# A gated mixer on one core: two x tiles and the first w_in blocks loaded in another order, and the left-over rows of the last four output tiles put in one 64-row stretch

## The chip, the core and the metric

The kernel runs on one core of a Trainium2 chip. The metric is the device time of one execution in microseconds (us); a kernel is run several times and the median counts. The profiles show one execution each. PE is TensorE's matmul stream and PEld its weight loads, DVE is VectorE, ACT is ScalarE, POOL is GpSimd, SP is SyncE. ACTq and SPq are the DMA issues of the ACT and SP queues.

## What is computed

S = 2048 rows, D = 512, F = 1376, half of it FH = 688, 32 heads of 16. All data are bf16. Cut to what matters:

```python
g = sigmoid((x * gate_w).sum(-1, keepdims=True))
# A: linear attention with softmax feature maps
q, k, v = split(x @ wqkv)
phi(t) = concat(softmax(t @ w_phi), softmax(-(t @ w_phi)))      # per head
a = (phi(q) @ (phi(k).T @ v)) / (phi(q) @ phi(k).sum(rows) + 1e-6) @ wo
# B: spatial gating
z = gelu(x @ w_in)
z1, z2 = z[:, :688], layernorm(z[:, 688:])
u = z1 * (w_sp @ z2 + b_sp[:, None])
b = u @ w_out
out = g * a + (1 - g) * b
```

## The kernel before

The 2048 rows are cut into 16 row tiles of 128. D is cut into four blocks of 128 (dt = 0..3), which TensorE contracts. `xT[:, dt, rows]` is x transposed, the stationary operand of nearly every matmul of the first half. The orders of PE and ACT are written out by hand (`tc.manual_schedule`), so both run in the order of the code; SP, POOL and DVE are ordered by the framework, in step with the code.

**Phase 1 (L321 to L338): z.** For each row tile, `z2_tile` multiplies x with the second half of w_in: eight matmuls (four dt, two column halves j of HF = 344 columns), accumulated in a two-bank PSUM tile `zp`. Column 344 of the second half is the gate logit, for which gate_w sits as a 689th column in `w_z2`. ACT then takes the gelu (L206). `z1_tile` does the same with the first half of w_in.

**The very beginning (`z2_first_two`, L215 to L257)** is written out apart, since nothing is in SBUF yet:

- L119 to L125 issue the first loads: SP takes x tile 0, then blocks dt = 0, 2, 3 of `w_z2`; ACT takes x tile 1 (so the two x tiles are loaded side by side), then block dt = 1, then gate_w into four rows of `gaterow`, which DVE has zeroed at L101.
- `warm_up` (L220) runs matmuls on constants into a bank that is overwritten later.
- `x_T` (L279) transposes blocks of an x tile on PE by a matmul with `ident`, and a copy on DVE (L287) or ACT (L284) takes them to `xT`.
- `one(tt, dt, j)` is one z matmul of row tile tt (L191). For j = 1 it is 345 columns wide, the gate's column among them.
- `gate_T` (L289) transposes gate_w on PE and DVE writes it into column 688 of all four blocks of `w_z2` (L292). A matmul that reads this column must wait for it.
- `z_part` (L229) does a part of the columns of half 1 for dt = 0: first 344 columns without the gate's, later that one column alone.

**Phase 2 (L573 to L595):** k, v, the key-value sums and the first halves of `w_sp @ z2` (`gg_half`, L452).

**Phase 3 (L597 to L608): output.** Step i of the loop does one `gg_half`, the attention of tile i + 1 (`attn_tile`, or `attn_tile_64` in 64-row matmuls), and `ba_step(i - 1)`, the output of a tile: `ba_attn` (four matmuls of 512 columns, from `oT`, L510) and `ba_spat` (five, from `uT`, L516), accumulated in one PSUM bank. u has 688 = 5*128 + 48 columns, so 48 left-over rows of its transpose remain. For them `uT` is padded, at one end for even tiles and at the other for odd ones, and `w_rem` holds the same 48 rows of w_out at its top and at its bottom, zeros between. `ba_rem` (L519) multiplies them: in the last step of a group of `BA_GROUPS` it runs once for each tile of the group, on rows 0 to 63 for even tiles and on rows 64 to 127 for odd ones (`halves`). Then `ba_store` scales each accumulator by 1 - g, on ACT (L531) or DVE (L527), and issues its DMA to `out`.

The groups are tiles 0-3, 4-7, 8-11 and 12-13. Tiles 14 and 15 come after the loop in `ba_tile` (L538): each does `ba_spat`, a `ba_rem` over all 128 rows, then `ba_attn`, then the store; tile 15 does so twice, for columns 0 to 383 and for columns 384 to 511. The PSUM banks of the outputs are four `acc_banks` in turn; `q_bank` and `g_bank` are two more, for `q_tile` and `gg_half`.

Of the kernel before, what the change touches and what calls it, by code (L numbers as in the profile page):

```python
# [14 lines left out]
P = 128  # L15
# [20 lines left out]
def kernel(  # L36
# [73 lines left out]
    for q in range(4):  # L110
        qs = slice(32 * q, 32 * q + 32)
        nc.vector.tensor_tensor(
            out=ident[qs, qs], in0=ramp[qs, 0, :], in1=ramp[qs, 1, :], op=ALU.is_equal)
    nc.gpsimd.memset(brow[:], 0.0)
    nc.gpsimd.memset(wphi[:], 0.0)
    def load_z2w(eng, dt):
        eng.dma_start(out=w_z2[:, dt, 0:FH], in_=w_in_v[:, dt, FH:F])

    nc.sync.dma_start(out=xs[:, 0, :], in_=x2[0:P, :])  # L119
    nc.scalar.dma_start(out=xs[:, 1, :], in_=x2[P:2 * P, :])  # L120
    load_z2w(nc.sync, 0)
    load_z2w(nc.scalar, 1)
    load_z2w(nc.sync, 2)
    nc.scalar.dma_start(out=gaterow[0:NDT, :], in_=gate_w.rearrange("(dt p) -> dt p", p=P))
    load_z2w(nc.sync, 3)  # L125
    scrap = early.tile([P, 1], BF16, name="scrap")
    nc.scalar.activation(
# [58 lines left out]
    def pq_tile(shape, dtype=FP32):  # L186
        return psF.tile(shape, dtype, name="pq", tag=next_turn("pq", 2))

    def z_one(zp, tt, wt, w, dt, j, skip=False):
        n = HF if j == 0 else w - HF  # L190
        nc.tensor.matmul(  # L191
            zp[:, j, 0:n], lhsT=xT[:, dt, tt * P:(tt + 1) * P],
            rhs=wt[:, dt, j * HF:j * HF + n],
            start=(dt == 0), stop=(dt == NDT - 1), skip_group_check=skip,
        )

    def z_mm(tt, wt, w):
# [17 lines left out]
    def z2_first_two():  # L215
        zps = [zp_tile() for _ in range(2)]
        tp1 = psA.tile([P, 2, P], BF16, name="tp1", tag=next_turn("zp", 3))
        turn["zp"] -= 1

        def warm_up(n, w=CH):  # L220
            for _ in range(n):
                nc.tensor.matmul(  # L222
                    zps[0][:, 1, 0:w], lhsT=nc.const_aps.tensor(1.0, [P, P], BF16),
                    rhs=nc.const_aps.tensor(1.0, [P, w], BF16), start=True, stop=True)

        def one(tt, dt, j):
            z_one(zps[tt], tt, w_z2, FH + 1, dt, j, skip=True)

        def z_part(tt, c0, c1, start):  # L229
            nc.tensor.matmul(  # L230
                zps[tt][:, 1, c0:c1], lhsT=xT[:, 0, tt * P:(tt + 1) * P],
                rhs=w_z2[:, 0, HF + c0:HF + c1], start=start, stop=False, skip_group_check=True)

        warm_up(6)
        warm_up(1, P)
        x_T(0, 0, 1, pq_tile([P, 1, P], BF16)[:, :, :])
        x_T(0, 1, NDT, pq_tile([P, 3, P], BF16)[:, :, :])
        x_T(1, 0, 2, tp1[:, :, :])
        x_T(1, 2, NDT, pq_tile([P, 2, P], BF16)[:, :, :], on_act=True)
        warm_up(2, P)  # L240
        one(0, 0, 0)
        z_part(0, 0, HF, True)
        one(0, 1, 0)
        one(1, 0, 0)
        gate_T()
        z_part(1, 0, HF, True)
        one(1, 1, 0)
        for tt in range(2):
            one(tt, 1, 1)
        for tt in range(2):  # L250
            one(tt, 2, 0)
            one(tt, 2, 1)
            z_part(tt, HF, HF + 1, False)
        for tt in range(2):
            one(tt, 3, 0)
            one(tt, 3, 1)
            z2_out(tt, zps[tt])  # L257
# [21 lines left out]
    def x_T(i, d0, d1, tp, on_act=False):  # L279
        for dt in range(d0, d1):  # L280
            nc.tensor.transpose(tp[:, dt - d0, :], xs[:, i, dt * P:(dt + 1) * P], ident[:, :])  # L281
        dst = xT[:, d0:d1, i * P:(i + 1) * P]
        if on_act:
            nc.scalar.copy(out=dst, in_=tp)  # L284
        else:
            with tc.high_priority():
                nc.vector.tensor_copy(out=dst, in_=tp)  # L287

    def gate_T():  # L289
        gt = pq_tile([P, NDT])  # L290
        nc.tensor.matmul(gt[:, :], lhsT=gaterow[:, :], rhs=ident[:, 0:NDT], start=True, stop=True)
        nc.vector.tensor_copy(out=w_z2[:, :, FH], in_=gt[:, :])  # L292
# [55 lines left out]
    def bank_tile(tag):  # L348
        return psM.tile([P, CH], FP32, name="mm", tag=tag)
# [158 lines left out]
    def ba_attn(acc, tt, start, stop, c0=0, c1=D):  # L508
        for g in range(NG):
            nc.tensor.matmul(acc, lhsT=oTs[tt][:, g, :], rhs=wo_t[:, g, c0:c1],  # L510
                             start=start and g == 0, stop=stop and g == NG - 1)

    def ba_spat(acc, tt, start, c0=0, c1=D):
        i = tt % 2
        for ft in range(5):
            nc.tensor.matmul(acc, lhsT=uTs[tt][:, i + ft, :], rhs=w_main[i][:, ft, c0:c1],  # L516
                             start=start and ft == 0, stop=False)

    def ba_rem(acc, tt, rows, stop, c0=0, c1=D):  # L519
        nc.tensor.matmul(  # L520
            acc, lhsT=uTs[tt][rows, 5 * (1 - tt % 2), :], rhs=w_rem[rows, c0:c1], start=False, stop=stop)

    def ba_store(acc, tt, c0, c1, on_dve):
        ob = work.tile([P, c1 - c0], BF16, name=f"ob{c1 - c0}", bufs=4 if c1 - c0 == D else 1)
        dst = out2[tt * P:(tt + 1) * P, c0:c1]
        if on_dve:
            nc.vector.tensor_scalar(  # L527
                out=ob[:, :], in0=acc, scalar1=g_inv[:, tt:tt + 1], scalar2=None, op0=ALU.mult)
            nc.sync.dma_start(out=dst, in_=ob[:, :])
        else:  # L530
            nc.scalar.activation(out=ob[:, :], in_=acc, func=AF.Copy, scale=g_inv[:, tt:tt + 1])  # L531
            nc.scalar.dma_start(out=dst, in_=ob[:, :])

    def acc_tile():
        acc_banks.append(acc_banks.pop(0))
        return bank_tile(acc_banks[-1])

    def ba_tile(tt, cuts=(0, D)):  # L538
        for h, (c0, c1) in enumerate(zip(cuts, cuts[1:])):
            acc = acc_tile()[:, 0:c1 - c0]  # L540
            ba_spat(acc, tt, True, c0, c1)
            ba_rem(acc, tt, slice(0, P), False, c0, c1)
            ba_attn(acc, tt, False, True, c0, c1)
            ba_store(acc, tt, c0, c1, h > 0)

    def ba_step(tt):
        group = next(g for g in BA_GROUPS if tt in g)
        accs[tt] = acc_tile()
        ba_attn(accs[tt][:, :], tt, True, False)
        ba_spat(accs[tt][:, :], tt, False)  # L550
        if tt == group[-1]:
            for t in group:
                ba_rem(accs[t][:, :], t, halves[t % 2], True)
            if tt + 2 < NT - 1:
                attn_tile_64(tt + 2)
            for t in group:
                ba_store(accs[t][:, :], t, 0, D, False)

    oTs = {}
    uTs = {}  # L560
    eqTs = {}
    accs = {}
    BA_GROUPS = [range(0, 4), range(4, 8), range(8, 12), range(12, 14)]
    Q_AT = (5, 7, 9, 11, 13, 15)
    ggs = [(tt, j) for tt in range(NT) for j in range(2)]

# [6 lines left out]
    with tc.manual_schedule(engines={mybir.EngineType.PE, mybir.EngineType.Activation}):  # L573
        ks = {0: k_tile(0)}
        kvacc = psM.tile([P, 8, P], FP32, name="kvacc", tag="kvat", bufs=1)
        pend = []
        for tt in range(NT):
            if tt + 1 < NT:
                ks[tt + 1] = k_tile(tt + 1)
            ek, rk = ks.pop(tt)  # L580
            pend.append((tt, ek, v_tile(tt, rk)))
            if len(pend) == 3:
                kv_acc(*pend.pop(0))
            gg_next(mm_tile())
            if tt == 7:
                w_main, w_rem, wo_t = load_out_weights()
            if tt in Q_AT:
                q_tile(Q_AT.index(tt), mm_tile())
        nc.scalar.activation(out=g_el[:, :], in_=glog[:, :], func=AF.Exp)
        nc.vector.tensor_scalar(out=g_1p[:, :], in0=g_el[:, :], scalar1=1.0, scalar2=None, op0=ALU.add)  # L590
        nc.vector.reciprocal(out=g_inv[:, :], in_=g_1p[:, :])
        for p_ in pend:
            kv_acc(*p_)
        kvz_evac()
        gg_next(mm_tile())  # L595
        nq = len(Q_AT)
        q_bank, g_bank, *acc_banks = [next_turn("mm", 6) for _ in range(6)]  # L597
        attn_tile(0)
        for i in range(NT - 1):
            if i + nq < NT:  # L600
                q_tile(i + nq, bank_tile(q_bank))
            gg_next(bank_tile(g_bank if i + nq < NT or i % 2 == 0 else q_bank))
            if i not in (4, 8, 12):
                attn_tile(i + 1)
            if i > 0:
                ba_step(i - 1)
        ba_tile(14)
        ba_tile(15, cuts=(0, 384, D))  # L608


# [28 lines left out]
```

The softmax here doesn't subtract the row's maximum and nothing guards it: scores larger than these inputs give would overflow.

## Time and profile before

| | us |
|---|---|
| median of 5 runs | 206.46 |
| lowest, highest | 206.21, 207.05 |
| the profiled execution | 206.21 |
| its span, first to last instruction | 204.5 |
| PE busy in it | 200.9 (98%) |
| PE weight loads | 120.2 (59%) |
| DVE, ACT, POOL busy | 129.6, 75.5, 45.6 |
| granted TensorE clock | 1.000 |

The page has the share of each engine, the span in 40 slices, the DMA queues, the chain of work that ended last, the groups of instructions by line, and the DMA issues with their median time to landing. Three further views are used: the timeline (instructions in order of time: start, duration of the piece, engine, line, operation, output and input, how many, and the idle time before it with what ended it), the chain of waits in order of time (start, length, what), and the answers for one tile, which give a DMA's time from issue to landing. [...]

### The profile page before, as it was taken

How to read it: one execution, taken by the hardware profiler on the slowest of the kernel's cores; microseconds unless marked ns; L12 is line 12 of the kernel's file. 1: busy time of each engine (PE TensorE's matmuls, PEld its weight loads, DVE VectorE, ACT ScalarE, POOL GpSimd, SP SyncE). 2: the span in 40 equal slices, each digit the busy share in tenths (PEclk: the TensorE clock that was granted, in tenths of full speed). 3: DMA queues.
4: the chain of work that ended last, by engine and by line, in shares of the span. 5: the costliest groups of instructions: out<-in, count | busy, mean ns of one | idle time of the engine just before them, and what ended most of it. 6: DMA issues, size and time to landing. Idle time of an engine off the chain costs nothing.

```text
span 204.5 us, 3998 instructions
## 1 busy us (share of the span) xinstructions
PE 200.9 (98%) x1559; PEld 120.2 (59%) x1559; DVE 129.6 (63%) x282; ACT 75.5 (37%) x123; POOL 45.6 (22%) x76
## 2 busy tenths in 40 slices
PE   8999999999999999999999999999999999999994
PEld 4666666655665555656565666555555555665642
DVE  4568484838977597979797689555566645633330
ACT  3566678795222333342424042222351126002222
POOL 3020202022523325424242442222204220200000
PEclk9999999999999999999999999999999999999999
DMA  6999799999999027941322229763557468542942
GB/s 201 254 212 147 87 145 282 182 290 221 250 258 204 3 38 195 275 93 23 69 53 40 51 38 119 150 120 70 98 157 80 91 114 181 68 96 53 148 89 79
DMA packets 89931, 27.22 MB, mean 133 GB/s; under 512 B 84184, under 2 KB 89912, under 8 KB 89912
## 3 DMA queue, kind: packets, MB, share of 16 engines
q1 hardware_dynamic: 87312, 24.59, 64.1%
q10 hardware_dynamic: 2600, 2.37, 4.3%
q8 instruction: 12, 0.20, 0.4%
q14 instruction: 7, 0.06, 0.1%
HBM read 4.15 MB, written 2.10 MB: 31 GB/s over the span
## 4 chain that ended last, share of the span: by engine, by line
PE 98%; DVE 0%; issue 0%
PE mm L455 37%; PE zp L191 18%; PE mm L356 14%; PE mm L516 9%; PE mm L510 7%; PE mm L396 7%; PE kvacc L412 2%; PE at L468 2%; PE zp L222 1%; PE mm L520 1%; PE zp L308 0%; PE at L479 0%; PE pq L281 0%; PE pq L308 0%; DVE ob L527 0%; PE zp L230 0%
## 5 line engine op out<-in xcount | busy, mean ns | idle before, releaser
L455 PE MATMUL mm<-z2all,wspT 128*128 128x344 bf16 x512 | 79.9, 309 | 0.0
L455 PEld LDWEIGHTS <-wspT 128*128 128x128 bf16 x512 | 49.0, 98 | 25.3
L191 PE MATMUL zp<-w_z,xT 128*128 128x344 bf16 (+1 forms) x254 | 38.1, 309 | 0.0
L360 ACT ACTIVATE eq<-mm 128x512 bf16<-128x512 f32 x32 | 17.4, 594 | 51.4 <-PE mm L356 25.7
L364 DVE TENSOR_REDUCE zs<-eq 128x64 f32<-128x1024 bf16 x16 | 19.5, 1220 | 20.1 <-ACT eq L360 20.1
L191 PEld LDWEIGHTS <-xT 128*128 128x128 bf16 x254 | 24.4, 98 | 12.0 <-issue 0.2
L360 ACT ACTIVATE ek<-mm 128x512 bf16<-128x512 f32 x32 | 17.3, 601 | 27.1 <-PE mm L356 27.1
L460 DVE SCALAR_TENSOR_TENSOR ucat<-mm,bT,z1all 128x344 bf16<-128x344 f32 x32 | 17.4, 544 | 15.1 <-PE mm L455 15.1
L373 POOL TENSOR_TENSOR eq<-eq,ratio 128x512 bf16<-128x512 bf16 x16 | 16.9, 1056 | 44.6 <-DVE ratio L372 36.6
L531 ACT ACTIVATE ob<-mm,g_inv 128x512 bf16<-128x512 f32 (+1 forms) x16 | 10.9, 680 | 32.4 <-PE mm L520 26.6
L364 DVE TENSOR_REDUCE zs<-ek 128x64 f32<-128x1024 bf16 x16 | 19.3, 1208 | 2.8 <-ACT ek L360 2.8
L516 PE MATMUL mm<-wspT,uT 128*128 128x512 bf16 (+2 forms) x85 | 20.1, 367 | 0.0
L356 PEld LDWEIGHTS <-xT 128*128 128x128 bf16 x128 | 12.2, 98 | 12.0
L373 POOL TENSOR_TENSOR ek<-ek,ratio 128x512 bf16<-128x512 bf16 x16 | 16.9, 1056 | 2.2 <-DVE ratio L372 1.7
L510 PE MATMUL mm<-wspT,oT 128*128 128x512 bf16 (+2 forms) x68 | 16.6, 366 | 0.0
L356 PE MATMUL mm<-wq_p,xT 128*128 128x512 bf16 x64 | 16.4, 379 | 0.0
L396 PE MATMUL mm<-wv_sb,xT 128*128 128x512 bf16 x64 | 16.4, 379 | 0.0
L356 PE MATMUL mm<-wk_p,xT 128*128 128x512 bf16 x64 | 16.3, 379 | 0.0
L209 DVE BATCH_NORM_STATS2 bn<-z2all 128x6 f32<-128x344 bf16 x32 | 14.9, 501 | 0.0
L206 ACT ACTIVATE z2all<-zp 128x688 bf16<-128x688 f32 x16 | 11.8, 743 | 7.3 <-PE zp L191 7.1
L261 ACT ACTIVATE z1all<-zp 128x688 bf16<-128x688 f32 x16 | 11.9, 743 | 5.1 <-PE zp L191 4.7
L516 PEld LDWEIGHTS <-uT 128*128 128x128 bf16 x85 | 8.1, 98 | 9.4 <-issue 0.2
(77 smaller groups left out, 143.0 us busy)
## 6 DMA issues: line engine op xcount, KB each, us to landing
out_dram<-ob ACTq DMA_DIRECT2D x15, 128.0 KB, 2.4
wspT<-in_B_w_out_dram SPq DMA_DIRECT2D x2, 640.0 KB, 4.9
w_z<-in_B_w_in_dram SPq DMA_DIRECT2D x2, 344.0 KB, 4.5
w_z<-in_B_w_in_dram SPq DMA_DIRECT2D x3, 172.0 KB, 3.3
wv_sb<-in_A_wqkv_dram SPq DMA_DIRECT2D x2, 256.0 KB, 2.8
wspT<-in_A_wo_dram SPq DMA_DIRECT2D x2, 256.0 KB, 4.0
uT<-ucat SPq DMA_TRANSPOSE x16, 2.8
eqT<-eq SPq DMA_TRANSPOSE x16, 3.9
```

Of the source, the lines that this page charges most:

```text
L191: nc.tensor.matmul(zp[:, j, 0:n], lhsT=xT[:, dt, tt * P:(tt + 1) * P], rhs=wt[:, dt, j * HF:j * HF + n], start=(dt == 0), stop=(dt == NDT ...
L209: nc.vector.bn_stats(out=bn6[:, tt, j, :], in_=z2v[:, j, :])
L261: nc.scalar.activation(out=z1all[:, tt, :].rearrange("p (j n) -> p j n", j=2), in_=zp[:, :, 0:HF], func=AF.Gelu_apprx_tanh,)
L356: nc.tensor.matmul(ps[:, :], lhsT=xT[:, dt, tt * P:(tt + 1) * P], rhs=w[:, dt, :], start=(dt == 0), stop=(dt == NDT - 1))
L360: nc.scalar.activation(out=e[:, :, a, :], in_=ps[:, :].rearrange("p (h f) -> p h f", f=DH), func=AF.Exp, scale=1.0 - 2.0 * a)
L364: nc.vector.tensor_reduce(out=z[:].rearrange("p h a -> p (h a)"), in_=e[:].rearrange("p h a f -> p (h a) f"), axis=AX.X, op=ALU.add,)
L373: nc.gpsimd.tensor_tensor(out=e[:, :, 1, :], in0=e[:, :, 1, :], in1=ratio[:, :, None].to_broadcast([P, H, DH]), op=ALU.mult)
L396: nc.tensor.matmul(v_ps[:, :], lhsT=xT[:, dt, tt * P:(tt + 1) * P], rhs=wv_sb[:, dt, :], start=(dt == 0), stop=(dt == NDT - 1))
L455: nc.tensor.matmul(gp[:, 0:HF], lhsT=wspT[:, st, tt * P:(tt + 1) * P], rhs=z2all[:, st, j * HF:(j + 1) * HF], start=(st == 0), stop=(st == ...
L460: nc.vector.scalar_tensor_tensor(out=ucat[tt % NU][:, c0 + j * HF:c0 + (j + 1) * HF], in0=gp[:, 0:HF], scalar=bT[:, tt:tt + 1], in1=z1all[ ...
L510: nc.tensor.matmul(acc, lhsT=oTs[tt][:, g, :], rhs=wo_t[:, g, c0:c1], start=start and g == 0, stop=stop and g == NG - 1)
L516: nc.tensor.matmul(acc, lhsT=uTs[tt][:, i + ft, :], rhs=w_main[i][:, ft, c0:c1], start=start and ft == 0, stop=False)
```

## The change

**At the beginning.** SP now loads x tile 0, then x tile 1, then blocks 2 and 3. ACT loads the first 344 columns of block 0, then block 1, then the other 344 columns of block 0. gate_w is loaded by the POOL queue, ahead of two memsets. Two 128-column warm-ups take the place of one after the six of 512 columns, and three and one of them stand further down in place of two. The first z matmul stands between the transposes of x tile 0 and those of x tile 1. The second half (j = 1) begins with dt = 1, without the gate's column; `gate_T` comes after that; dt = 0 follows, and the gate's single column is done for dt = 0 and 1 after `one(tt, 2, 1)`, which is the first matmul to read it.

**At the end.** The last group is tiles 12 to 15. `ba_step(14)` does attention and `ba_spat` of tile 14 as for other tiles; then the left-over rows of tiles 12, 13, 14 and of the two pieces of tile 15 are done in one row, in 64-row matmuls; those of tile 15 begin its accumulators (the second piece in `q_bank`). Tiles 12, 13 and 14 are scaled by ACT, DVE and ACT, and all three are stored through the SP queue. Then each piece of tile 15 does `ba_spat`, `ba_attn` and its store, as before on ACT (ACT queue) and DVE (SP queue).

```diff
+    nc.gpsimd.dma_start(out=gaterow[0:NDT, :], in_=gate_w.rearrange("(dt p) -> dt p", p=P))
     nc.gpsimd.memset(brow[:], 0.0)
     nc.gpsimd.memset(wphi[:], 0.0)
...
     nc.sync.dma_start(out=xs[:, 0, :], in_=x2[0:P, :])
-    nc.scalar.dma_start(out=xs[:, 1, :], in_=x2[P:2 * P, :])
-    load_z2w(nc.sync, 0)
+    nc.scalar.dma_start(out=w_z2[:, 0, 0:HF], in_=w_in_v[:, 0, FH:FH + HF])
+    nc.sync.dma_start(out=xs[:, 1, :], in_=x2[P:2 * P, :])
     load_z2w(nc.scalar, 1)
     load_z2w(nc.sync, 2)
-    nc.scalar.dma_start(out=gaterow[0:NDT, :], in_=gate_w.rearrange("(dt p) -> dt p", p=P))
+    nc.scalar.dma_start(out=w_z2[:, 0, HF:FH], in_=w_in_v[:, 0, FH + HF:F])
     load_z2w(nc.sync, 3)
...
         warm_up(6)
-        warm_up(1, P)
+        warm_up(2, P)
         x_T(0, 0, 1, pq_tile([P, 1, P], BF16)[:, :, :])
         x_T(0, 1, NDT, pq_tile([P, 3, P], BF16)[:, :, :])
+        warm_up(3, P)
+        one(0, 0, 0)
         x_T(1, 0, 2, tp1[:, :, :])
         x_T(1, 2, NDT, pq_tile([P, 2, P], BF16)[:, :, :], on_act=True)
-        warm_up(2, P)
-        one(0, 0, 0)
-        z_part(0, 0, HF, True)
         one(0, 1, 0)
+        warm_up(1, P)
         one(1, 0, 0)
-        gate_T()
-        z_part(1, 0, HF, True)
         one(1, 1, 0)
         for tt in range(2):
-            one(tt, 1, 1)
+            z_part(tt, 1, 0, HF, True)
+        gate_T()
         for tt in range(2):
-            one(tt, 2, 0)
+            z_part(tt, 0, 0, HF, False)
+        one(0, 2, 0)
+        one(1, 2, 0)
+        for tt in range(2):
             one(tt, 2, 1)
-            z_part(tt, HF, HF + 1, False)
+            for dt in range(2):
+                z_part(tt, dt, HF, HF + 1, False)
         for tt in range(2):
             one(tt, 3, 0)
             one(tt, 3, 1)
...
-    def ba_rem(acc, tt, rows, stop, c0=0, c1=D):
+    def ba_rem(acc, tt, start=False, c0=0, c1=D):
+        rows = halves[tt % 2]
         nc.tensor.matmul(
-            acc, lhsT=uTs[tt][rows, 5 * (1 - tt % 2), :], rhs=w_rem[rows, c0:c1], start=False, stop=stop)
+            acc, lhsT=uTs[tt][rows, 5 * (1 - tt % 2), :], rhs=w_rem[rows, c0:c1], start=start, stop=not start)
...
             nc.scalar.activation(out=ob[:, :], in_=acc, func=AF.Copy, scale=g_inv[:, tt:tt + 1])
-            nc.scalar.dma_start(out=dst, in_=ob[:, :])
+            (nc.sync if on_sp else nc.scalar).dma_start(out=dst, in_=ob[:, :])
...
-    def ba_tile(tt, cuts=(0, D)):
-        for h, (c0, c1) in enumerate(zip(cuts, cuts[1:])):
-            acc = acc_tile()[:, 0:c1 - c0]
-            ba_spat(acc, tt, True, c0, c1)
-            ba_rem(acc, tt, slice(0, P), False, c0, c1)
-            ba_attn(acc, tt, False, True, c0, c1)
-            ba_store(acc, tt, c0, c1, h > 0)
+    def ba_last():
+        last = NT - 1
+        ba_step(last - 1)
+        pieces = [(acc_tile()[:, 0:384], 0, 384), (bank_tile(q_bank)[:, 0:P], 384, D)]
+        for t in BA_GROUPS[-1][:-1]:
+            ba_rem(accs[t][:, :], t)
+        for acc, c0, c1 in pieces:
+            ba_rem(acc, last, True, c0, c1)
+        for n, t in enumerate(BA_GROUPS[-1][:-1]):
+            ba_store(accs[t][:, :], t, on_dve=n == 1, on_sp=True)
+        for n, (acc, c0, c1) in enumerate(pieces):
+            ba_spat(acc, last, False, c0, c1)
+            ba_attn(acc, last, False, True, c0, c1)
+            ba_store(acc, last, c0, c1, on_dve=n == 1)
...
-    BA_GROUPS = [range(0, 4), range(4, 8), range(8, 12), range(12, 14)]
+    BA_GROUPS = [range(0, 4), range(4, 8), range(8, 12), range(12, 16)]
...
-        ba_tile(14)
-        ba_tile(15, cuts=(0, 384, D))
+        ba_last()
```

More of the change, by code (lines that the diff above doesn't have):

```diff
@@ L187, in pq_tile, with z_one @@
         return psF.tile(shape, dtype, name="pq", tag=next_turn("pq", 2))
-    def z_one(zp, tt, wt, w, dt, j, skip=False):
+    def z_one(zp, tt, wt, w, dt, j, first=0):
         n = HF if j == 0 else w - HF
@@ L193, in z_one @@
             rhs=wt[:, dt, j * HF:j * HF + n],
-            start=(dt == 0), stop=(dt == NDT - 1), skip_group_check=skip,
+            start=(dt == first), stop=(dt == NDT - 1), skip_group_check=first > 0,
         )
@@ L226, in one, with z_part @@
         def one(tt, dt, j):
-            z_one(zps[tt], tt, w_z2, FH + 1, dt, j, skip=True)
-        def z_part(tt, c0, c1, start):
+            z_one(zps[tt], tt, w_z2, FH + 1, dt, j, first=j)
+        def z_part(tt, dt, c0, c1, start):
             nc.tensor.matmul(
-                zps[tt][:, 1, c0:c1], lhsT=xT[:, 0, tt * P:(tt + 1) * P],
-                rhs=w_z2[:, 0, HF + c0:HF + c1], start=start, stop=False, skip_group_check=True)
+                zps[tt][:, 1, c0:c1], lhsT=xT[:, dt, tt * P:(tt + 1) * P],
+                rhs=w_z2[:, dt, HF + c0:HF + c1], start=start, stop=False, skip_group_check=True)
         warm_up(6)
-        warm_up(1, P)
+        warm_up(2, P)
         x_T(0, 0, 1, pq_tile([P, 1, P], BF16)[:, :, :])
         x_T(0, 1, NDT, pq_tile([P, 3, P], BF16)[:, :, :])
+        warm_up(3, P)
+        one(0, 0, 0)
         x_T(1, 0, 2, tp1[:, :, :])
         x_T(1, 2, NDT, pq_tile([P, 2, P], BF16)[:, :, :], on_act=True)
-        warm_up(2, P)
-        one(0, 0, 0)
-        z_part(0, 0, HF, True)
         one(0, 1, 0)
+        warm_up(1, P)
         one(1, 0, 0)
-        gate_T()
-        z_part(1, 0, HF, True)
         one(1, 1, 0)
         for tt in range(2):
-            one(tt, 1, 1)
+            z_part(tt, 1, 0, HF, True)
+        gate_T()
         for tt in range(2):
-            one(tt, 2, 0)
+            z_part(tt, 0, 0, HF, False)
+        one(0, 2, 0)
+        one(1, 2, 0)
+        for tt in range(2):
             one(tt, 2, 1)
-            z_part(tt, HF, HF + 1, False)
+            for dt in range(2):
+                z_part(tt, dt, HF, HF + 1, False)
         for tt in range(2):
@@ L517, in ba_spat, with ba_store @@
                              start=start and ft == 0, stop=False)
-    def ba_rem(acc, tt, rows, stop, c0=0, c1=D):
+    def ba_rem(acc, tt, start=False, c0=0, c1=D):
+        rows = halves[tt % 2]
         nc.tensor.matmul(
-            acc, lhsT=uTs[tt][rows, 5 * (1 - tt % 2), :], rhs=w_rem[rows, c0:c1], start=False, stop=stop)
-    def ba_store(acc, tt, c0, c1, on_dve):
+            acc, lhsT=uTs[tt][rows, 5 * (1 - tt % 2), :], rhs=w_rem[rows, c0:c1], start=start, stop=not start)
+    def ba_store(acc, tt, c0=0, c1=D, on_dve=False, on_sp=False):
         ob = work.tile([P, c1 - c0], BF16, name=f"ob{c1 - c0}", bufs=4 if c1 - c0 == D else 1)
@@ L552, in ba_step @@
             for t in group:
-                ba_rem(accs[t][:, :], t, halves[t % 2], True)
-            if tt + 2 < NT - 1:
-                attn_tile_64(tt + 2)
+                ba_rem(accs[t][:, :], t)
+            attn_tile_64(tt + 2)
             for t in group:
-                ba_store(accs[t][:, :], t, 0, D, False)
+                ba_store(accs[t][:, :], t)
     oTs = {}
```

## The prediction

> **What bounds the kernel now.** I read the page's chain first: does one engine carry the span from start to end?
>
> ```profile
> PE 98%; DVE 0%; issue 0%
> ```
>
> It does, and the granted clock is 1.000, so every nanosecond taken from or added to PE's stream moves the end, unless the last matmul isn't what ends last. Other engines, POOL and DMA matter only where PE waits for them or behind its last matmul. So I looked for waits of PE in the two places that the change touches. First the chain of waits and the timeline of the first 7 us:
>
> ```profile
> 4.43 0.11 PE zp L222 x2
> 4.54 0.28 PE zp L191
> ...
> 5.26 0.17 PE zp L230
> 5.43 0.88 PE zp L191 x5
> 6.30 0.00 PE zp L230
> ```
>
> ```profile
> 3.81 0.68 DVE L287 COPY xT<-pq 128x128 bf16<-128x128 bf16 x2 [1.50 <-PE pq L281]
> 4.40 0.28 DVE L287 COPY xT<-tp 128x256 bf16<-128x256 bf16 x1
> 4.51 0.31 PE L191 MATMUL zp<-w_z,xT 128*128 128x344 bf16 x1
> ...
> 5.09 0.17 PE L291 MATMUL pq<-ident,gaterow 128*128 128x4 bf16 x1
> ...
> 5.33 0.17 DVE L292 CAST w_z<-pq 128x4 bf16<-128x4 f32 x1 [0.64 <-PE pq L291]
> ```
>
> Two small holes are to be seen. The first z matmul starts at 4.51, though its weight load was at 4.32 and the two warm-ups ahead of it started at 4.26 and 4.31: it waits for block 0 of w_z2, issued by SP at 1.27, whose kind lands after 3.2 us, at 4.47. That costs 0.14. And five z matmuls take 0.88 instead of 5 * 0.146 = 0.73 (0.146 is the step of L191: 4.51, 4.66, 4.80, 4.95): the first that reads the gate's column waits until DVE has written it (5.33 + 0.17 = 5.50) and starts at 5.56. That costs 0.15. After 5.56 the stream is dense; the last matmul of the two tiles starts at 6.92, so tile 2 begins at 7.07.
>
> Then the end, in the chain of waits:
>
> ```profile
> 187.07 0.54 PE mm L520 x4
> 187.61 0.19 PE at L479 x16
> 187.80 2.44 PE mm L455 x16
> ...
> 196.97 0.32 PE mm L520 x2
> 197.30 1.19 PE mm L516 x5
> 198.48 0.22 PE mm L520
> 198.70 0.86 PE mm L510 x4
> 199.56 0.81 PE mm L516 x5
> 200.37 0.16 PE mm L520
> 200.54 0.65 PE mm L510 x4
> ...
> 201.78 0.35 DVE ob L527
> ```
>
> Four 64-row L520 of 512 columns take 0.54, two take 0.32: so a pair (upper and lower half) costs 0.22, what one full-height matmul costs (198.48), and entering the stretch 0.11. Leaving it costs 0.11 more: the 16 of L455 take 2.44 instead of the 2.33 of other steps, the five of L516 1.19 instead of 1.08. PE's last matmul ends at 201.76; DVE scales until 202.13, SP issues the store at 202.16, it lands after 1.5 us at 203.66, the span ends at 204.5.
>
> **The end, part by part.** Before, from 196.97: 0.32 + 1.19 + 0.22 + 0.86 + 0.81 + 0.16 + 0.65 + 0.28 + 0.06 + 0.24 = 4.79. After: attention of tile 14 0.86, its ba_spat 1.08, entering 0.11, the rems 0.43 (12 beside 13; 14, 512 columns, beside the two pieces of 15, 384 + 128), leaving 0.11, then 0.81 + 0.65 for the first piece and 0.28 + 0.24 for the second: 4.57. PE saves **0.22 us**: the three full-height rems of tiles 14 and 15 (0.22 + 0.16 + 0.06) against one more pair. The number of mode changes stays.
>
> Is anything late for the new order? Tile 14's oT, issued at 192.0 and landed after 2.7, is wanted at 196.97 now, not 198.70: 2.3 us of room. Tile 15's uT (195.42 + 2.7 = 198.1) is wanted by its rem at about 199.2; its oT (196.73 + 2.5 = 199.2) at 200.37, not 200.54. q_bank was last read by DVE at 190.9. All hidden, the nearest by 1.1 us.
>
> The stores of tiles 12 to 14 come later and closer. Their sums are ready at 199.4 (12, 13) and 199.6 (before: ACT starts 0.36 after the first L520). ACT takes 0.69 each without the 0.34 of a DMA issue between, so 12 and 14 are done at 200.1 and 200.8, before piece one (201.05). DVE takes 13: no row has 512 columns of this form; between 0.35 (128 columns, L527) and 0.75 (L491, 512 and two inputs) I take 0.7, done by 200.2, long before piece two. SP issues them at 0.37 each at 200.1, 200.5 and 200.85, is free at 201.2, and takes the last piece at 201.94 (201.54 + 0.02 + 0.35 + 0.03). Behind SP's three nothing else waits but that store. It lands at 203.44, ACT's 96 KB (issued 201.66, 1.7) at 203.36, so the 0.22 reaches the end. The bounds: a 128 KB store landed between 1.7 and 3.4 us after its issue in this trace; by 3.4, tile 14's would land at 204.25 and set the end, 0.6 later than before; the three after 197 had 1.7 to 1.8 with no transposes in flight, as here, and by that it is 202.6. Taken: -0.22; range -0.25 to +0.6.
>
> **The beginning, part by part.** Warm-ups: one 128-column matmul more ahead of the transposes, at 0.107 a step in this stretch, where weight loads take 152 ns and not yet 98. x tile 0 landed by 3.35 (0.80 + 2.4 = 3.2), so PE is what sets the first transpose: 3.57 instead of 3.46. Its four end at 4.2, and three warm-ups fill until 4.27. DVE copies block 0 0.35 after the transpose, for 0.23: 4.15. The half of block 0 is first on ACT, at 0.80; the 128 KB x tiles took 2.4 to 2.5, so 88 KB are there by 3.3. So the first z matmul starts at about **4.27** instead of 4.51: the wait for w goes.
>
> What is late next is x tile 1. Its transposes now stand behind that matmul: 4.42, 4.47, 4.53, 4.58 (0.054 a step from here, as five 128-column matmuls took 0.28 at 201.19). SP issues it second, at 1.27, landing at 3.8: no wait. But DVE is at the other three blocks of tile 0 from 4.24 to 4.60, and the pair for tile 1, transposed at 4.47 and drained at 4.70, is copied from 4.73 to 5.01. one(0, 1, 0) fits in at 4.70 (its block of w, ACT's second again, landed at 4.65 before, behind more bytes), a warm-up behind it; one(1, 0, 0) can load its weights at 5.05 and starts at **5.10**. The fill of 4.91 to 5.10 is a new hole. From 5.10 there are 14 z matmuls (14 * 0.146 = 2.04), the gate's transpose (0.03, 5.09 to 5.12) and four single columns instead of two (0.03 each, 0.12): 7.29, against 7.07. The gate wait is gone, since four matmuls (0.58) now stand between the transpose at 5.69 and the first reader, and the hand-over took 0.47. The late blocks are in time: second half of block 0, third on ACT at about 1.7, 3.3 to land, 5.0, wanted at 5.72; block 2 at 5.0, wanted at 6.0.
>
> So the beginning **loses 0.22**: before, six matmuls had started by 5.27 and both holes together cost 0.29; the new order spends that and more on the wait for the copy of x tile 1, the added warm-ups and two single columns. Bounds: without any wait for the copy, PE's own work would put one(1, 0, 0) at 4.83 (-0.05 in all); with 0.1 lost at two hand-overs more, +0.42.
>
> **gate_w by POOL** isn't in the trace. DVE's zeroing of its rows ends at 0.99, so it is issued at about 1.0; two memsets of 0.73 wait behind it, whose readers come past 14 us. Loads of the first stage land between 1.9 (2 KB) and 6.9 us (a transposed x chunk): at 2.9 to 7.9. Nearest are the x tiles, in the same microsecond, at 2.5: 3.5. It is wanted at 5.69, so it costs nothing; by the far end 2.2. [...]
>
> **Sum** for the profiled execution: 206.21 + 0.22 - 0.22 = 206.2. The median of the five stands 0.25 above it, so: **206.4**, no change.
>
> **The rivals.** (1) *Faster, 205.7.* The first loads bound the median run more than the profiled one: if they land 0.8 later, before waits 0.8 longer for its 172 KB block, after only where its 88 KB exceed 4.27, and 0.22 of the end comes on top. For it: the 0.14 wait at 4.51 exists. Against: the runs lie within 0.84 in all, and the lowest is this one.
> (2) *Slower, 207.5.* gate_w through POOL lands after 5.69; PE's queue is in order, so gate_T holds everything and each us late is a us. It decides from 5.69 on; over the bound from 6.3; at 6.8 the price is 1.1. For it: no row for POOL, the far end 7.9. Against: 2.2 us of room by the nearest row.
> (3) *Slower, 207.2.* The three stores crowded on SP land by the 3.4 us row, the end is 0.54 later than before in place of earlier, and 0.22 from the beginning adds up. For it: 480 KB to write in 2 us. Against: DMA is at 28 to 41% busy there.
> (4) The rems don't pair (15's pieces in line behind 14): 0.22 back at the end, 206.7, still no change; part of the forecast.
>
> **How the numbers follow.** Forecast 0.62, (1) 0.13, (2) 0.14, (3) 0.11. What this kernel's measurement can tell from no change is about 0.3%, 0.62 us. Some of the forecast's own spread (-0.3 to +0.4, with the runs' 0.3) crosses that. Faster 0.17, same 0.58, slower 0.25. The forecast alone holds 205.9 to 207.0; with the bounds of the stores 205.9 to 207.2.
>
> **What would show it.** The first L191 at 4.27, the second row tile's first at 5.10 behind DVE's copy, tile 2 at 7.29; L520 in one piece of 0.54 near 199; PE's last matmul 4.57 after ba_spat of tile 13; last store issued on SP. Wrong if tile 2 begins before 7.0 or the gate's transpose stands with PE idle ahead of it.

## The result and the profile after

The changed kernel ("after") takes 206.99 us in the median of 44 runs (206.34 to 207.31), before 206.63 in 75 (206.10 to 209.34). The ratio is **1.0013, with a 95% interval of 1.0006 to 1.0019**: about 0.27 us slower (the means of the two lists differ by 0.26, the medians by 0.36), a small loss that is clear of noise where no change was forecast. One execution of before, 209.34, and one of e1 below, 209.22, stand far above all others of their kernels and are left out of the ratios. The profiled execution took 206.63 with a span of 204.9; that of before, 206.21 and 204.5.

The page's chain is what it was, PE from end to end:

```profile
PE 98%; DVE 0%; issue 0%
```

The beginning of after, in the chain of waits (start, length, what):

```profile
4.21 0.32 PE zp L223 x3
4.53 0.29 PE zp L192
4.81 0.20 PE tp L285 x2
5.01 0.02 issue
5.04 0.30 DVE xT L291
5.34 0.05 issue
5.39 0.47 PE zp L192 x2
```

and in the timeline (line numbers have moved: L192 is the z matmul, L291 the copy of a transposed x tile, L295 and L296 the gate):

```profile
4.32 0.49 PE L192 MATMUL zp<-w_z,xT 128*128 128x344 bf16 x1
...
5.04 0.29 DVE L291 COPY xT<-tp 128x256 bf16<-128x256 bf16 x1 [0.44 <-PE tp L285]
...
5.38 0.11 PEld L192 LDWEIGHTS <-xT 128*128 128x128 bf16 x2 [0.33 <-DVE xT L291]
...
5.98 0.17 PE L295 MATMUL pq<-ident,gaterow 128*128 128x4 bf16 x1
...
6.22 0.18 DVE L296 CAST w_z<-pq 128x4 bf16<-128x4 f32 x1 [0.89 <-PE pq L295]
```

The first z matmul is early, at 4.32 instead of 4.51, and no wait for w is left there (its half of block 0 landed at 3.47). But the chain then leaves PE: it runs through DVE's copy of x tile 1, and the weight load behind it waits 0.33. PE's stream stands for 0.24 of it: the warm-up at 5.10, worth 0.055 in full stride, is followed only at 5.39. That is the hole whose end the prediction put at 5.10. The matmul at 4.32 takes 0.49, one in full stride 0.31 (in before L191's last 0.309 each and start 0.146 apart, so two that follow each other overlap): PE still ran at half its pace, until about 4.85, while in the profile of before the pace doubled at 4.2 (the last weight load of 152 ns ends at 4.87 and at 4.25). Tile 2 starts at 7.60 instead of 7.07.

The end of after, in the chain of waits:

```profile
196.41 1.08 PE mm L520 x5
197.49 0.86 PE mm L514 x4
198.35 1.08 PE mm L520 x5
199.43 0.54 PE mm L525 x4
199.97 0.92 PE mm L520 x5
200.89 0.65 PE mm L514 x4
201.54 0.28 PE mm L520 x5
201.82 0.24 PE mm L514 x4
...
202.08 0.35 DVE ob L532
```

From the last ba_spat of tile 13 (197.49) to PE's last matmul (202.05) it is 4.56, before 4.79. The middle is the same in both: from tile 2 to that ba_spat 189.90 before (7.07 to 196.97) and 189.89 after. So the 0.42 between the two executions is +0.53 from the beginning, -0.23 from the end, and +0.13 behind PE's last matmul: 206.63 - 202.05 = 4.58 against 206.21 - 201.76 = 4.45.

A useful yardstick follows for all runs below: **the moment at which ba_spat of tile 13 ends** (196.97 before, 197.49 after) shows what the beginning cost, and what comes behind it is the end. It must be read beside the moment at which PE's pace doubles. The three profiles with the beginning of before lie near one line: 196.85 for a doubling at 3.85 (f4), 196.97 at 4.2 (before), 197.62 at 5.7 (e1), so each us of delay costs 0.43. Interpolated on it, before would end ba_spat of tile 13 at 197.25 for a doubling at 4.85, and after, with 197.49, loses 0.24 at the same moment. This is an estimate from four profiles.

### The profile page after: what moved, and what is told of

Read it like the earlier page. It is cut to its first block, busy times and chain, and to the rows that moved or that the text cites. A ratio compares the mean times of both kernels' runs of the same rounds, so it can differ in the third digit from the quotient of the medians.

```text
span 204.9 us, 4014 instructions
## 1 busy us (share of the span) xinstructions
PE 201.1 (98%) x1564; PEld 120.4 (59%) x1564; DVE 130.5 (64%) x283; ACT 74.6 (36%) x122; POOL 46.4 (23%) x77
## 4 chain that ended last, share of the span: by engine, by line
PE 98%; DVE 0%; issue 0%
PE mm L459 36%; PE zp L192 18%; PE mm L360 14%; PE mm L520 8%; PE mm L514 7%; PE mm L400 7%; PE kvacc L416 2%; PE at L472 2%; PE zp L223 2%; PE mm L525 1%; PE zp L312 0%; PE zp L231 0%; PE at L483 0%; PE pq L285 0%; PE pq L312 0%; DVE ob L532 0%
## 5 line engine op out<-in xcount | busy, mean ns | idle before, releaser
L192 PE MATMUL zp<-w_z,xT 128*128 128x344 bf16 x252 | 38.1, 310 | 0.1
L192 PEld LDWEIGHTS <-xT 128*128 128x128 bf16 x252 | 24.3, 98 | 12.0 <-DVE xT L291 0.3
L536 ACT ACTIVATE ob<-mm,g_inv 128x512 bf16<-128x512 f32 (+1 forms) x15 | 10.1, 680 | 33.1 <-PE mm L525 28.5
```

The costliest lines, as they stand in the source:

```text
L192: nc.tensor.matmul(zp[:, j, 0:n], lhsT=xT[:, dt, tt * P:(tt + 1) * P], rhs=wt[:, dt, j * HF:j * HF + n], start=(dt == first), stop=(dt == ...
```

## The experiments

The theory, "order": the new order of PE waits for the copy of x tile 1 and has more small matmuls. Rivals: "late half block" (the split block 0 and the loads behind it land late), "clock" (only the moment at which PE's pace doubles, which is chance), "POOL queue" and "crowded stores". Each ratio is to before on the same chip, with its 95% interval.

**Each half of the change by itself.** The code is cut between `z2_first_two` and `z1_tile`; one file has the old part above and the new below, the other the reverse.

> The beginning of before with the end of after (one 64-row stretch for tiles 12 to 15). Theory 'order': the loss is all in the beginning, so this is before minus 0.22 us (PE from the last ba_spat of tile 13 to its end 4.56 instead of 4.79), ratio about 0.999. Rival 'end': the time from PE's last matmul to the end of the span grew by 0.11 (2.74 to 2.85) because of the crowded stores, so only about 0.1 is gained, ratio about 0.9995.

> The beginning of after with the end of before. Theory 'order': the first two row tiles cost 0.25 to 0.3 more whatever the moment at which PE's step halves, ratio about 1.0013 to 1.0025 with what the end no longer gives. Rival 'clock': the 0.53 of the profiled execution is chance, since PE's step halved at 4.85 there and at 4.2 in the profile of before; then this is before plus 0.0 to 0.1, and the profile's tile 2 start moves with the moment of the halving alone.

e1: 0.9996 (0.9984 to 1.0009), which holds both of its expectations. e2: 1.0036 (1.0022 to 1.0050), 207.36 against 206.63. The loss is in the beginning. e2 is above the range that I gave for "order" (its interval reaches down into it): its profile has, beside 0.15 for the copy of x tile 1, a second wait of 0.5 behind gate_T, for the second half of block 0, which landed at 6.5.

**gate_w back to ACT.**

```diff
-    nc.gpsimd.dma_start(out=gaterow[0:NDT, :], ...)
...
     nc.scalar.dma_start(out=w_z2[:, 0, HF:FH], in_=w_in_v[:, 0, FH + HF:F])
+    nc.scalar.dma_start(out=gaterow[0:NDT, :], ...)
```

> After, with gate_w loaded by the ACT queue as its fourth load instead of by POOL. gate_w landed at 5.02 from POOL and PE took it at 5.98 without a wait, so theory 'order' expects no change from after, within 0.05 us, before plus 0.27. Rival 'POOL queue': POOL's own DMA slows the other first loads (blocks 2 and 3 took 3.8 to 4.3 to land instead of 3.3) or adds a wait at the end of the program (0.11 more after PE's last matmul); then this is 0.1 or more faster than after.

1.0041 (1.0026 to 1.0056), five runs between 207.31 and 207.65. Neither expectation: it isn't faster, and it is slower than after. In its profile PE's pace doubles only at 6.6, at half pace no wait is left, and ba_spat of tile 13 ends at 198.16. Blocks 2 and 3 landed 3.8 and 3.9 us after their issue, as in after, so POOL's load isn't what delays them. Why all five runs took so long stays open. The chip may have a part in it: e2, e3 and e4, all on the chip of this comparison, lie at 1.0022 to 1.0041, and after itself (f2) and its variants on three other chips (e5, e6, e8, e9, f1) at 1.0003 to 1.0014.

**x tile 1 transposed first.** In after, the two `x_T(1, ...)` go back ahead of `warm_up(3, P)` and `one(0, 0, 0)`.

> After, with the transposes of x tile 1 put back ahead of the first z matmul, nothing else changed. Theory 'order': the copy of x tile 1 comes early enough, the hole of 0.24 ahead of one(1, 0, 0) is gone and the beginning is 0.2 to 0.3 shorter than in after: about before minus 0.1. Rival 'clock': the order costs nothing by itself, and this is after within 0.05.

1.0022 (1.0008 to 1.0035). The wait for the copy is gone, but nothing is gained. The chain of waits and the timeline of this run say where it went:

```profile
1.74 4.62 DMA w_z<-in_B_w_in_dram
6.36 0.04 issue
6.40 0.45 PE zp L231 x2
```

```profile
5.54 0.18 PE L295 MATMUL pq<-ident,gaterow 128*128 128x4 bf16 x1
6.40 0.45 PE L231 MATMUL zp<-w_z,xT 128*128 128x344 bf16 x2 [0.68 <-DMA w_z<-in_B_w_in_dram]
```

The second half of block 0, ACT's third load, is issued at 1.74 and lands after 4.62 us; PE stands from about 5.57 to 6.40. In after the same load landed at 6.00 and its reader started at 6.04, 0.03 later than an unbroken stream: the first wait hid nearly all of the second.

**The late half block taken away, in two ways.** e5 loads block 0 whole as ACT's first load; e6 does that and transposes x tile 1 first; e8 leaves the loads and uses the second half of dt = 0 last:

```diff
-        for tt in range(2):
-            z_part(tt, 0, 0, HF, False)
         one(0, 2, 0)
         one(1, 2, 0)
         for tt in range(2):
             one(tt, 2, 1)
-            for dt in range(2):
-                z_part(tt, dt, HF, HF + 1, False)
-        for tt in range(2):
-            one(tt, 3, 0)
-            one(tt, 3, 1)
+            z_part(tt, 1, HF, HF + 1, False)
+        one(0, 3, 0)
+        one(1, 3, 0)
+        for tt in range(2):
+            z_part(tt, 0, 0, HF + 1, False)
+            one(tt, 3, 1)
```

> After, with block 0 of w_z2 loaded whole as ACT's first load, so that ACT has no third load. Theory 'late half block': the second half of block 0 landed at 6.0 to 6.6 in the runs so far, PE stood up to 0.85 ahead of its first reader (z_part of dt = 0), and that sets the beginning in most executions; with it gone the median is 0.2 to 0.4 below after, near before, and blocks 2 and 3 land 3.3 to 3.5 after their issue as in before, not 3.8 to 4.6. Rival 'copy': the hole ahead of one(1, 0, 0) (0.24, x tile 1 copied late) is all of it; then this equals after within 0.1.

> As the kernel before in this call (block 0 whole, first on ACT), and the transposes of x tile 1 put back ahead of the first z matmul. 'Late half block' and 'copy' both: neither hole is left, tile 2 starts at 7.1 to 7.2 when PE's step halves at 4.2, the end gives 0.22: median 0.1 to 0.2 below before. 'Copy' alone: 0.25 below after and not below before.

> After's loads, order of the matmuls changed alone: the second half of dt = 0 is used after dt = 2 and half of dt = 3 instead of ahead of them, two single columns fewer. 'Late half block': PE has 6 other matmuls (0.9) while that half lands, so the wait is gone wherever it was; median 0.2 to 0.4 below after, still above or at before because blocks 2 and 3 land late too (5.5 to 6.7). 'Copy': as after within 0.1.

1.0003 (0.9989 to 1.0016), 1.0009 (0.9995 to 1.0024) and 1.0004 (0.9991 to 1.0016). Times of a dozen runs, spread over 1 us each, don't tell these apart from after; the profiles do. In e8 the wait for the half block is gone and 0.24 for the copy is left. But the two matmuls taken from behind gate_T were also what covered the gate's hand-over: gate_T starts at 5.49, DVE has written the column at 5.91, and the first matmul that reads it starts at 5.96, 0.15 later than an unbroken stream. It is the wait for the gate's column that the change had removed. In e5 no wait is left, but its pace doubled at 6.65 and hides them. In e6 x tile 1, second on SP, landed at 4.30 (1.26 + 3.04) and PE stood 0.4 for it: the order that wants x tile 1 early needs it loaded beside x tile 0, as before did (landed at 3.35). Blocks 2 and 3 landed after 3.9 and 3.8 in e5, 3.3 and 3.4 in e6: the split isn't shown to be what delays them.

**The best of both, by the sum.** Before's loads, and before's order up to dt = 1; from there the gate's column is taken out of the matmuls of dt = 1 and both first halves of dt = 2 come ahead of its first reader, as in after; after's end; run twice (e10 is the same kernel).

```diff
         for tt in range(2):
-            one(tt, 1, 1)
+            z_part(tt, 1, 0, HF, False)
+        one(0, 2, 0)
+        one(1, 2, 0)
         for tt in range(2):
-            one(tt, 2, 0)
             one(tt, 2, 1)
-            z_part(tt, HF, HF + 1, False)
+            for dt in range(2):
+                z_part(tt, dt, HF, HF + 1, False)
```

> The loads and the order of before in the beginning, with only the gate's column taken out of the matmuls of dt = 1 (done later as single columns, as in after), and the end of after. The wait of 0.15 for the gate's column goes, two single columns cost 0.06, the end gives 0.22: 0.2 to 0.3 below before, ratio 0.9985 to 0.999, if the end's gain holds and the beginning's loss is in the loads and the order of x tile 1. If the gate's wait is hidden whenever PE's step halves late, only 0.15 to 0.2.

> The same kernel as e7_gate_late_end (before's loads and order, gate column later, end of after), a second time, since one of its runs was 209.06 and hid the rest. 0.2 to 0.3 below before by the sum; 0.1 or less if the gate's wait was hidden in most runs.

e7: 0.9997 (0.9974 to 1.0020), with the profiled execution at 209.06. e10: 1.0003 (0.9994 to 1.0011). Half of it holds: the wait for the gate's column is gone. But in e10 the first matmul of tile 2 waits instead, for its own x:

```profile
PEld L191 <- DMA xT<-in_A_x_dram: 0.4, 1, 0.4
```

The transposing load of x tiles 2 and 3, issued at 2.67, landed at 7.2 there (6.5 in the profile of before), and PE's stream stands 0.23, more than the 0.15 saved. So the saving of the gate's wait has cover of less than 0.6 us of DMA and is given back when the load is late.

**Old loads, new order.** After with the three changed load lines of before.

> After, with the first loads of before (x tile 1 first on ACT, block 0 whole, second on SP, gate_w third on ACT): the order of PE is after's. Theory 'loads': no wait at the second half of block 0 is left, and x tile 1 is there early; what remains of the order is the wait for block 0 at the first z matmul (4.47) and for the copy of x tile 1 behind it (0.1 to 0.2): tile 2 starts at about 7.3 for a half step until 4.2, the median 0.1 to 0.3 below after. Rival 'order': the waits for the copy are the loss, and it is as slow as after within 0.1.

1.0014 (1.0003 to 1.0026), ba_spat of tile 13 at 197.47, pace doubled at 4.85, as in after (197.49 and 4.85). The same hole of 0.24. "Loads" fails as the sole cause: with the old loads the new order and the new end together are as slow as the whole change, within wide intervals, and the two profiles, equal in the moment of doubling, differ by 0.02. e10 beside it on the same chip has old loads and nearly the old order: 206.56 against 206.71, and 197.11 at a pace doubled at 4.45 (0.17 of the 0.36 between 197.11 and 197.47 is that earlier moment, by the line above).

**A quieter beginning**, to see the end without the noise of the pace: both x tiles loaded after `w_z1`, `warm_up(27)` instead of 6, once with each end.

> Before, with both x tiles loaded after the two big w_z1 loads and 27 warm-ups instead of 6, so that PE is kept busy until about 8 to 9.6 us and its step has halved (3.5 to 6.7 in the runs so far) before the first transpose. It is 4 to 6 us slower on purpose. Theory 'half step by chance': the runs now lie within about 0.4 us of each other instead of 1.2. Rival 'the spread comes from elsewhere' (loads, the end): they still spread over 1 us.

> The same beginning with the end of after. With the noise of the half step out of the way, the end alone: theory 'the whole gain reaches the end': 0.2 to 0.25 below the run beside it with the end of before. Rival 'crowded stores': 0.1 or less below it.

q1: 1.0258 (1.0239 to 1.0276), 211.49 to 212.42. q2: 1.0282 (1.0245 to 1.0319), 211.37 to 214.11. The runs did not draw together, so this misses: either the pace isn't the only source of the spread, or late loads brought a new one. What it gives is the pair of profiled executions, whose beginnings agree within 0.03: 211.56 and 211.44. PE's end is 0.18 earlier (207.11, 206.93); 0.12 reaches the time, between the two expectations.

**Two fillings together, and the last repeats.** f1 is e8 with one line more: the matmul of tile 0 for dt = 1, second half, in place of the warm-up ahead of `one(1, 0, 0)`. f2 is after itself; f3 is before with gate_w on POOL; f4 is e1 again.

```diff
         one(0, 1, 0)
-        warm_up(1, P)
+        z_part(0, 1, 0, HF, True)
         one(1, 0, 0)
```

> After's loads and its end, with the two idle stretches of PE filled by other matmuls: the half-1 matmul of row tile 0 with dt = 1 stands ahead of one(1, 0, 0) in place of the warm-up (fills the wait for the copy of x tile 1), and the second half of dt = 0 is used last (its late block). Theory 'order': tile 2 starts 0.25 to 0.35 earlier than in after for the same moment of the half step, about 7.2 to 7.3; time before -0.05 to +0.05, and 0.2 to 0.3 below after beside it. Rival 'loads': the first blocks come later with after's plan, whatever the order; then it is within 0.1 of after.

> After, unchanged, for a comparison on the same chip and a second profile of it. Before plus 0.27. The hole ahead of one(1, 0, 0) is there again (0.15 to 0.25 if the step has halved by then, none if not), while the moment of the halving and the landing of block 0's second half (6.0 to 6.6) are others.

> Before, with gate_w loaded by POOL, nothing else changed. Theory 'POOL costs at the end of the program': from PE's last matmul to the end of the execution 4.54 instead of 4.45 (SP's last wait for the other engines 0.7 instead of 0.6), so before plus 0.1. Gate's landing: about 5.0, while gate_T stands at about 5.0 in this order, so a wait of 0 to 0.3 there would show too: before plus 0.1 to 0.4.

> The same kernel as e1_end_only (beginning of before, end of after), again, for the end's gain in total time: PE saves 0.23, of which 0.05 to 0.1 is lost between PE's last matmul and the end; before minus 0.13 to 0.18.

f1: 1.0004 (0.9992 to 1.0016), 206.77. f2: 1.0004 (0.9990 to 1.0019), 206.99, before beside them 206.76. f3: 1.0010 (0.9998 to 1.0022). f4: **0.9985 (0.9973 to 0.9998)**, 206.41, the only version with its interval below 1. f2's profile has both waits (0.15 for the copy, 0.3 for the half block, which landed at 6.30); ba_spat of tile 13 ends at 197.78. f1's does not wait for the half block, and has 197.16: 0.33 below after and 0.62 below f2, though the medians of f1 and f2 differ by 0.2 only and the intervals overlap. Most of the 0.33 is the pace, which doubled at 4.35 in f1; on the line of before f1 lies 0.13 above it, after 0.24, so 0.1 is what the filling gave. Its holes are not closed either:

```profile
4.85 0.31 PE L231 MATMUL zp<-w_z,xT 128*128 128x344 bf16 x1
5.14 0.11 PEld L192 LDWEIGHTS <-xT 128*128 128x128 bf16 x2 [0.33 <-DVE xT L289]
5.14 0.47 PE L192 MATMUL zp<-w_z,xT 128*128 128x344 bf16 x2
...
5.59 0.17 PE L293 MATMUL pq<-ident,gaterow 128*128 128x4 bf16 x1
5.62 0.74 PE L192 MATMUL zp<-w_z,xT 128*128 128x344 bf16 x3
5.83 0.17 DVE L294 CAST w_z<-pq 128x4 bf16<-128x4 f32 x1 [0.74 <-PE pq L293]
6.06 0.10 PEld L231 LDWEIGHTS <-xT 128*128 128x128 bf16 x1 [0.20 <-issue]
```

The matmul put in takes 0.146, and the next starts 0.29 behind it: 0.15 is still lost to the copy of x tile 1. Of the three behind gate_T the last reads the gate's column; they take 0.74 where an unbroken stream takes 0.60, so the wait of 0.15 for that column is there as in e8. That tile 2 would start 0.25 to 0.35 earlier at the same moment of doubling is not met.

f3 shows gate_w through POOL in an order that wants it early:

```profile
L114 POOL DMA_DIRECT2D gaterow<-in_gate_w_dram x1: 763/763/763, 1.4 to 1.4; - x1
...
  DMA gaterow<-in_gate_w_dram: 0.2, 1
...
DMA to landing us min/median/max: 4.0/4.0/4.0
```

It is issued at 1.4 and lands at 5.4. The weight load of gate_T waited 0.2 for it, but behind a matmul at half pace: PE's stream lost nothing there (5.395 to 5.681 is the half-pace step of 0.286). In before gate_T started at 5.09, so at full pace this order would wait 0.3 or more, an estimate. In after, where gate_T comes at 5.98, it costs PE nothing.

**What lies behind PE's last matmul.** SP's own waits at the very end of the program (times of all, how many, the longest), of before, then f4 (new end), then e2 (old end, gate_w on POOL), then after (both):

```profile
SPq L634 <- DMA out_dram<-ob: 0.7, 1, 0.7
SPq L634 <- PEq L634: 0.6, 2, 0.4
```

```profile
SPq L640 <- DMA out_dram<-ob: 0.9, 2, 0.6
...
SPq L640 <- PEq L640: 0.6, 2, 0.4
```

```profile
SPq L638 <- DMA out_dram<-ob: 0.7, 1, 0.7
SPq L638 <- PEq L638: 0.7, 2, 0.5
```

```profile
SPq L644 <- DMA out_dram<-ob: 0.8, 2, 0.6
SPq L644 <- PEq L644: 0.7, 2, 0.5
```

The view lists waits over 0.15 only. In before SP waits for two stores as well, ACT's and then, for 0.12, its own; with the new end the first of the two that are listed is the store of tile 14, and that one delays nothing, since ACT's lands after it. What the landings of the last stores show is this: SP issues its last store 0.4 behind PE's last matmul in every profile; it lands 1.49 after its issue in before and 1.50 in q1, 1.50 and 1.51 in f3 and e2, and 1.54 to 1.61 with the new end (thirteen profiles; in e3 no landing is recorded). That the three stores ahead of it on SP delay it is the likely reason; it was not tried. And from that landing to the end of the span it is 0.83 to 0.85 in the eight profiles without POOL's load, 0.90 to 0.98 in the nine with it.

From PE's last matmul to the end of the execution it is 4.45 in before and q1, 4.54 and 4.58 with POOL's load alone (e2, f3), 4.49 to 4.63 with the new end alone (seven profiles, mean 4.55), and 4.57 to 4.70 with both (seven, mean 4.62).

## Why the prediction was wrong, step by step

1. **PE at the end: right.** 4.79 to 4.56, where 4.57 was worked out; one stretch of 0.54, leaving it 0.11.
2. **"So the 0.22 reaches the end": a step that failed.** Of PE's 0.23, 0.1 is lost behind PE: 4.45 becomes 4.55 in the mean. Each of SP's three stores landed after 1.8, as predicted (of the three after 197 that this was taken from, the trace of before records two landings, 1.76 and 1.72, the first with tile 15's oT in flight until 199.26); but the last piece's store, taken at the 1.5 of before, landed 0.05 to 0.11 later behind them. In after ACT's store of piece one is issued at 202.19, 0.14 behind PE's last matmul, before it was 0.07 (201.83 and 201.76), but it landed at 203.84, ahead of SP's at 204.00. Rival (3), 3.4 us to land, and rival (4), rems that don't pair, did not occur.
3. **gate_w by POOL "costs nothing": failed by 0.1.** It was issued at 1.42, not 1.0, behind the two memsets that the text puts after it, and landed at 5.07, not 3.5, still ahead of its reader at 5.98; in e2 it landed at 5.86, ahead of its reader at 6.00 by 0.15 only. What I left out is the end of the program, 0.09 to 0.13 longer in e2 and f3 than in before. Items 2 and 3 together are a term that the sum had at nothing: 4.45 becomes 4.62 in the mean, 0.17. Over the nine profiles with this load it landed at 4.8 to 5.9; what sets that moment was not shown. Rival (2) did not occur.
4. **"From 4.91 to 5.10 is a new hole": right, with a size that depends on the pace.** It was 0.24 in after, e9 and e8, 0.15 in f2, e2 and, with other filling, f1, and none in e3 and e5, where PE was at half pace and reached the spot later.
5. **"Second half of block 0 ... 5.0, wanted at 5.72": the other step that failed.** It landed at 5.7 in e8 and f1, 5.9 in e3, 6.0 in after, 6.3 in f2, 6.4 in e4 and 6.5 in e2. I took the 3.3 us of before's whole blocks, the second, third and fourth loads of SP. With after's plan of loads the third of ACT needs 3.9 to 4.8, though it is half a block, and blocks 2 and 3, still third and fourth on SP, need 3.5 to 4.6: a row of the old plan didn't hold for the new one. The wait was 0.8, 0.5 and 0.3 in e4, e2 and f2, and 0.03 in after's own profile. e9, without a third block on ACT, is no faster, so this wait isn't the whole loss.
6. **The pace of PE taken from one profile.** I worked both sums with the doubling at 4.2. In seventeen of the eighteen profiles it came between 3.5 and 6.8 (e7's later still), and after's own had it at 4.85. About 0.3 of the 0.53 in the pair of profiles is that (0.65 later, at 0.43 for each us); before's beginning pays too when it comes late (e1: 5.7 and 197.62), so this is chance and no cost of the change. What remains, 0.24 in after and 0.22 in e9, is the 0.22 that the prediction gave the beginning; in f2 and e2, doubled at 5.05 and 5.1, it is about 0.4 and 0.6, as the late half block adds to it.

In sum, the 0.22 at the beginning and PE's 0.23 at the end are right where no block is late, and they would cancel. They don't, because 0.17 is added behind PE's last matmul, and because the half block is late, by 0.03, 0.3 and 0.5 in the three profiles with after's beginning (after, f2, e2). For the two profiles of after, 0.24 and 0.4 at the beginning, less 0.23, with 0.17 more, make 0.2 and 0.3, an estimate; the ratio gives 0.27 (0.12 to 0.39). The range held, the sign did not. Of the 0.6 between the forecast of 206.4 and the 206.99 measured, 0.17 is before's own median, 206.63 over 75 runs against 206.46 over five. Three things stay open: how often the half block is late and what share of the median's loss it has, since times of a dozen runs don't resolve 0.2 us and neither e5, e8 nor f1 is shown to be faster than after; what sets the landing of blocks 2 and 3, which took 3.5 to 4.6 with after's load plan and 3.3 to 4.0 with before's (e7 apart); and why e3 is slower than after.

## What to carry to other kernels

When an order written by hand is packed so that one wait goes, list for every operand the moment it is wanted beside its own landing, measured with the new plan of loads where that changes too, since a row of the old plan can be 1 us off (4.3 for 3.3 here): a wait that is removed uncovers the next late operand, as e4 (0.8), e8 (0.15) and e10 (0.23) show. A profile is one execution; a sum of tenths of a microsecond in the first microseconds needs a few of them, since the moment at which PE reaches its full pace moved the result here by more than the edit (e1 and f4, one kernel, 5.7 and 3.85: 0.77 apart at ba_spat of tile 13; the edit 0.27). And time won on the last engine of the chain should be followed through the last store and the end of the program before it is counted: here 0.1 of 0.23 was lost there.

## What the runs showed of the hardware that was not expected

**PE's pace at the start.** The granted clock reads 1.000 from the beginning (before and after, each stretch of 2 us up to 6), yet until some moment a 128-column matmul takes 0.107 from start to start and its weight load 152 ns; afterwards 0.055 and 98 ns. The moment differs between executions of the same kernel: 4.85 and 5.05 (after, f2), 5.7 and 3.85 (e1, f4), 9.7 and 4.45 (e7, e10). Over seventeen profiles it spreads by 3.3, from 3.5 to 6.8. The earliest, 3.5 in e8, came 2.7 us after PE's first matmul at 0.84. What sets it was not shown.

**An idle stretch before it.** In e7's profile block 0 landed late, and PE waited for it:

```profile
4.42 0.15 PEld L191 LDWEIGHTS <-xT 128*128 128x128 bf16 x1
5.54 0.10 PEld L230 LDWEIGHTS <-xT 128*128 128x128 bf16 x1 [0.98 <-issue]
...
9.09 2.93 PEld L191 LDWEIGHTS <-xT 128*128 128x128 bf16 x19
```

PE was at half pace ahead of the gap of 0.98, and behind it most weight loads take 0.15 until 9.65, four us more. The execution took 2.4 us longer than the median of that kernel's other runs (209.06 against 206.60). It is one execution; that the gap is the cause of the long half pace was not tried.
